# Weighing the tile that two heads share: two half-width passes replaced by two full-width passes on TensorE

## The chip, the cores and the metric

The kernel runs on one core of a Trainium2 chip. The metric is the device time of one execution in microseconds (us), the median of three runs. The engines of the core are TensorE (PE for its matmuls, PEld for its weight loads), VectorE (DVE), ScalarE (ACT), GpSimd (POOL) and SyncE (SP, which issues the DMAs). Each engine works through its own instructions in order, and waits for others by semaphores.

## What is computed

Attention with queries that are pooled over neighbouring rows, then two feed-forward layers, all with float32 inputs. Batch is 4, with 8 heads, 1152 keys and queries of 64 elements per head; pooling by 2 leaves 576 query rows per head. Cut to what matters:

```python
q_pool = q.reshape(B, H, S // 2, 2, D).mean(axis=3)
scores = (1 / sqrt(D)) * q_pool @ k.transpose(0, 1, 3, 2)
attn = exp(scores - max(scores)); attn = attn / (sum(attn) + 1e-9)
x = attn @ v                       # then (B*576, H*64) = (2304, 512)
h = x @ w_in;  x = (h * cos(h)) @ w_out          # layer 1, d_ff 2048
h = x @ w_in2; out = (h * sigmoid(h)) @ w_out2   # layer 2, d_ff 2048
```

## The kernel before

Float32 operands are split in two float16 parts, high and low, and products of the parts are summed in PSUM. Attention goes by pairs of heads (j and j + 4) of one batch: 16 pairs. The 576 rows of a head are four tiles of 128 rows and a rest of 64; the rests of the two heads are put together in one tile, number 8 (`2 * NT`), with the first head in partitions 0 to 63 and the second in 64 to 127. So a pair has nine tiles, 144 in all, of which 16 are shared ones.

A tile goes through these steps. `tile_scores` makes the scores on TensorE into PSUM tiles `sp` (L391, and for the shared tile L399, which uses half of the array's columns for each head). `tile_exp` moves them to `sc` on DVE (L410), with the row's extreme `nb` (L415), and applies the exponential on ACT (L418). `tile_hi` and `tile_lo` split the weights in `hl` (L424 on ACT, L429 on POOL), and a transposing DMA brings them to `hlT` (L431), of which there are four buffers. `tile_pv` multiplies them with the values `vt` on TensorE, in 9 chunks of 128 keys: L442 the high part with both parts of v (2 x 65 = 130 columns), L446 the low part with v's high part (65 columns). Column 64 of v's high part is one, so it gathers the sum of the weights.

Three tiles make a group and share one PSUM tile `pv`, which has a single buffer: [128, 3, 2, 65]. A pair has three groups, and the shared tile is always in the second of them. After a group's last tile, `group_end` reads `pv` on DVE: the denominators (`den`, L454), then the sum of the two halves of each slot into SBUF (`pvs`, L460), then the reciprocal (L458), which reads only `den`. Then ACT scales the rows from `pvs` into `x32`, or into `xrem` for the shared tile (L465, three instructions a group). The next group's first matmul waits until `pv` has been read.

In the shared tile, the loop of L440 takes first the 64 columns of `hlT` that belong to the first head, with that head's v, into partitions 0 to 63 of `pv`, then the other 64 columns into partitions 64 to 127. Its matmuls stand in the trace as 128*64, against 128*128 of all others but L399's.

Between the steps of attention, generators that are advanced tile by tile put in other work: loads and splitting of the next pair, splitting of the feed-forward weights, and from the fifth pair on the matmuls of layer 1 (`h`, L522; `y`, L582). The order in which each engine runs all this is set when the kernel is built: a scheduler with its own costs takes whatever has become ready, by priorities. So matmuls of different steps alternate on TensorE. After the last pair come the rest of layer 1 and the splitting of the second layer's weights, and then layer 2 (`h`, L522; `o`, L603).

## Time and profile before

| what | before |
|---|---|
| runs | 1415.83, 1414.32, 1410.59 us; median 1414.32 |
| profiled execution, first to last instruction (span) | 1411.7 us, 24909 instructions |
| attention, by the first and the last weighing matmul | 48.6 to 859.2 us |
| layer 2, TensorE without a pause of note | 1021 to 1411.7 us |

The page's time of the profiled execution is its span; the table of runs lists no other time for that execution. The median of the runs is 2.6 us above the span. In a timeline, each row gives the start, the duration, the engine, the line and the operation; a matmul's duration includes its way through the array, so what one costs its engine is the distance from its start to the next one's start.

### The profile page before, as it was taken

To read this page: it belongs to the slowest core of one execution; us is meant where nothing else is said; L and a number is where in the kernel's file an instruction comes from. 1 tells how busy PE (TensorE), PEld (TensorE's weight loads), DVE (VectorE), ACT (ScalarE), POOL (GpSimd) and SP (SyncE) were. 2 spreads that over 40 slices of the span, in tenths; PEclk is the share of its full clock that TensorE was granted. 3 is DMA by queue.
4 is the path that set the end of the run, shared out by engine and by line. 5 is a ranking of instruction groups with operands and counts; after the bars stand their busy time and mean duration, and the time that the engine had idled before them with its cause. 6 is when DMAs were issued, how large, how long until landed. Compare 5 with 4: busy or idle time off the path is not lost. (4 is left out here: it accounts for less than half of the span.)

```text
span 1411.7 us, 24909 instructions
## 1 busy us (share of the span) xinstructions
PE 1164.1 (82%) x10020; PEld 853.2 (60%) x10020; DVE 988.5 (70%) x1848; ACT 768.7 (54%) x907; POOL 568.2 (40%) x296
## 2 busy tenths in 40 slices
PE   1465356787897768898889889978899999999998
PEld 0243233475675556666667678867776666666664
DVE  7999997678678888977999985999933322223221
ACT  3686487668777678777788785555421111111110
POOL 1577276535656466646666563553600000000000
PEclk9966568799999899999999999989999999999999
DMA  7799789987799999989999964544110000000001
GB/s 232 190 238 213 186 157 206 202 167 137 149 194 171 198 205 205 176 156 185 156 208 182 220 131 86 147 120 129 52 60 31 31 6 25 31 31 16 16 2 29
DMA packets 493075, 186.17 MB, mean 132 GB/s; under 512 B 433056, under 2 KB 467872, under 8 KB 492960
## 3 DMA queue, kind: packets, MB, share of 16 engines
q1 hardware_dynamic: 492960, 184.59, 61.9%
q8 instruction: 78, 1.28, 0.4%
q14 instruction: 37, 0.30, 0.1%
HBM read 66.58 MB, written 9.44 MB: 54 GB/s over the span
## 5 line engine op out<-in xcount | busy, mean ns | idle before, releaser
L429 POOL TENSOR_TENSOR hl<-sc,hl 128x1152 f16<-128x1152 f32 x144 | 368.7, 2569 | 194.0 <-ACT hl L424 109.8
L391 PE MATMUL sp<-kT,qT 128*128 128x512 f16 (+1 forms) x768 | 196.2, 373 | 112.0 <-DVE sc L410 85.9
L535 ACT ACTIVATE hk<-h,ca 128x512 f32<-128x512 f32 x144 | 97.9, 682 | 318.0 <-PE h L522 318.0
L522 PEld LDWEIGHTS <-ih 128*128 128x128 f16 x2304 | 227.3, 100 | 66.9 <-issue 7.3
L410 DVE TENSOR_SCALAR_CACHE_REDUCE sc<-sp,psu 128x512 f32<-128x512 f32 (+1 forms) x288 | 229.0, 807 | 48.1 <-PE sp L391 46.8
L418 ACT ACTIVATE sc<-sc,nb 128x1152 f32<-128x1152 f32 x144 | 179.9, 1250 | 91.0 <-DVE nb L415 78.2
L442 PE MATMUL pv<-vt,hlT 128*128 128x130 f16 (+1 forms) x1440 | 196.1, 238 | 37.4 <-DMA hlT<-hl 29.6
L522 PE MATMUL h<-ys,ih 128*128 128x256 f16 x1152 | 196.2, 273 | 1.0 <-ACT hk L535 1.0
L522 PE MATMUL h<-xT,ih 128*128 128x256 f16 x1024 | 190.6, 280 | 2.1 <-ACT hk L535 1.3
L442 PEld LDWEIGHTS <-hlT 128*128 128x128 f16 (+1 forms) x1440 | 148.0, 111 | 67.3 <-DMA hlT<-hl 39.5
L446 PE MATMUL pv<-vt,hlT 128*128 128x65 f16 (+1 forms) x1440 | 188.4, 208 | 0.0
L391 PEld LDWEIGHTS <-qT 128*128 128x128 f16 x768 | 78.0, 110 | 180.0 <-issue 138.5
L424 ACT ACTIVATE hl<-sc 128x1152 f16<-128x1152 f32 x144 | 165.3, 1155 | 23.4 <-DMA hlT<-hl 12.2
L570 DVE TENSOR_SCALAR gh<-hk,ck 128x1024 f16<-128x1024 f32 x36 | 27.0, 751 | 206.2 <-PE o L603 198.6
L582 PE MATMUL y<-gl,oh 128*128 128x256 f16 x576 | 158.4, 275 | 2.9 <-POOL gl L563 2.9
L582 PE MATMUL y<-gh,oh 128*128 128x256 f16 x576 | 158.4, 275 | 2.1 <-ACT y L591 2.1
L582 PE MATMUL y<-gh,ol 128*128 128x256 f16 x576 | 158.4, 275 | 0.0
L522 PE MATMUL h<-ys,il 128*128 128x256 f16 x576 | 157.0, 273 | 0.0
L446 PEld LDWEIGHTS <-hlT 128*128 128x128 f16 (+1 forms) x1440 | 143.3, 108 | 15.9 <-issue 6.0
L522 PE MATMUL h<-xT,il 128*128 128x256 f16 x512 | 143.1, 280 | 0.0
L522 PEld LDWEIGHTS <-il 128*128 128x128 f16 x1152 | 114.4, 99 | 18.0 <-issue 1.3
L582 PEld LDWEIGHTS <-oh 128*128 128x128 f16 x1152 | 112.5, 99 | 20.1 <-issue 4.2
(283 smaller groups left out, 2024.5 us busy)
## 6 DMA issues: line engine op xcount, KB each, us to landing
wst<-in_moe_w_in_dram SPq DMA_DIRECT2D x16, 1024.0 KB, 5.9
wst<-in_moe_w_out_dram SPq DMA_DIRECT2D x16, 1024.0 KB, 5.9
stk<-in_k_dram SPq DMA_DIRECT2D x32, 288.0 KB, 4.3
stv<-in_v_dram SPq DMA_DIRECT2D x32, 288.0 KB, 4.4
stq<-in_q_dram SPq DMA_DIRECT2D x32, 256.0 KB, 3.1
ydr<-y SPq DMA_DIRECT2D x9, 512.0 KB, 2.9
y32b<-ydr SPq DMA_DIRECT2D x9, 512.0 KB, 3.2
out_dram<-osb SPq DMA_DIRECT2D x16, 256.0 KB, 2.1
```

The costliest lines, as they stand in the source:

```text
L391: nc.tensor.matmul(sp[:, o - a:o - a + n], P.qT[e][:, t, :], kT[:, o:o + n], start=(e == 0), stop=(e == 1))
L410: nc.vector.tensor_scalar(out=T.sc[:, a:z], in0=sp, scalar1=T.P.su, scalar2=None, op0=ALU.mult, op1=ALU.min, accum_out=mx[:, x:x + 1],)
L418: nc.scalar.activation(out=T.sc, in_=T.sc, func=AF.Exp, scale=-1.0, bias=nb)
L424: nc.scalar.activation(out=hi, in_=T.sc, func=AF.Copy)
L429: nc.gpsimd.tensor_tensor(out=T.hl[:, 1, :], in0=T.sc, in1=T.hl[:, 0, :], op=ALU.subtract)
L442: nc.tensor.matmul(G.pv[r, T.gi], T.hlT[:, 0, c, r], P.vt[i][:, c], start=(c == 0), stop=(c == KC - 1), skip_group_check=True,)
L446: nc.tensor.matmul(G.pv[r, T.gi, 0], T.hlT[:, 1, c, r], P.vt[i][:, c, 0], start=False, stop=(c == KC - 1), skip_group_check=True,)
L522: nc.tensor.matmul(hp, wt[:, c, f * 128:(f + 1) * 128], xt(c), start=(i == 0), stop=(i == 3 * NC - 1), skip_group_check=True,)
L535: nc.scalar.activation(out=o, in_=blk.hp, func=AF.Copy if first else AF.Silu, scale=blk.c.a[:, g:g + 1])
L570: nc.vector.tensor_scalar(out=gh, in0=hk, scalar1=blk.c.k, scalar2=None, op0=ALU.mult)
L582: nc.tensor.matmul(blk.y[:, oc, :], wt[:, f, oc * 128:(oc + 1) * 128], gt[:, f % 4, :], start=(f == 0 and e == 0 and oc % 2 == 0), stop=(f ...
```

## The change

The shared tile is weighed as the other tiles are, with all 128 columns of `hlT`, once with the first head's v and once with the second's. The two results go to the two halves of its slot in `pv`, where other tiles have their two partial sums. In each result only the 64 rows of its own head are wanted. The three products (high with high, high with low, low with high) are now three matmuls of 65 columns for each chunk and head, summed in one place: 54 matmuls instead of 36.

The denominators are taken for both halves of each slot (6 instead of 3 columns). ACT scales the shared tile's rows straight from `pv` in PSUM, in two instructions of 64 rows each, instead of one of 128 rows from `pvs`. The other tiles keep their matmuls; their lines now are L450 and L454, the shared tile's L443, the scaling L473 and, for the shared tile, L478.

```diff
-        hs = [(slice(0, 128), t // NT)] if t < 2 * NT else [(slice(0, 64), 0), (slice(64, 128), 1)]
-        for r, i in hs:
-            for c in range(KC):
-                nc.tensor.matmul(
-                    G.pv[r, T.gi], T.hlT[:, 0, c, r], P.vt[i][:, c],
-                    start=(c == 0), stop=(c == KC - 1), skip_group_check=True,
-                )
-                nc.tensor.matmul(
-                    G.pv[r, T.gi, 0], T.hlT[:, 1, c, r], P.vt[i][:, c, 0],
-                    start=False, stop=(c == KC - 1), skip_group_check=True,
-                )
+        if t == 2 * NT:
+            for i in range(2):
+                for c in range(KC):
+                    for e, z in ((0, 0), (0, 1), (1, 0)):
+                        nc.tensor.matmul(
+                            G.pv[:, T.gi, i], T.hlT[:, e, c], P.vt[i][:, c, z],
+                            start=(c == 0 and e == 0 and z == 0), stop=(c == KC - 1 and e == 1),
+                            skip_group_check=True,
+                        )
+            return
...
-        den = small.tile([128, GT, 1], F32, tag="den", name="den", bufs=2)
+        den = small.tile([128, GT, 2, 1], F32, tag="den", name="den", bufs=2)
...
-                nc.scalar.activation(out=dst[:, i], in_=sm[:, o + i], func=AF.Copy, scale=den[:, o + i])
+                nc.scalar.activation(out=dst[:, i], in_=sm[:, o + i], func=AF.Copy, scale=den[:, o + i, 0])
+        if 2 * NT in G.tiles:
+            o, dst = G.tiles.index(2 * NT), xrem[:, G.P.b, G.P.j * D:(G.P.j + 1) * D]
+            for i in range(2):
+                r = slice(i * 64, (i + 1) * 64)
+                nc.scalar.activation(out=dst[r], in_=G.pv[r, o, i, 0:D], func=AF.Copy, scale=den[r, o, i])
```

The scheduler runs anew, so the order moves on all engines. Three places of the twelfth pair show it (pairs are counted from 0 in the prediction: pair 11). On TensorE, inside the shared tile, before the change (`hlT` is loaded as the weights, 64 columns of it; L582 is layer 1):

```order
L446 MATMUL pv<-vt,hlT 64x65
L442 LDWEIGHTS hlT
L442 MATMUL pv<-vt,hlT 64x130
L582 LDWEIGHTS oh_83
L582 MATMUL y<-gh,oh_83 128x256
L446 LDWEIGHTS hlT
L446 MATMUL pv<-vt,hlT 64x65
L582 LDWEIGHTS oh_83
L582 MATMUL y<-gl,oh_83 128x256
```

And after the change, at the end of the first stretch of the same tile (L391 makes scores):

```order
L443 LDWEIGHTS hlT
L443 MATMUL pv<-vt,hlT 128x65
L443 LDWEIGHTS hlT
L443 MATMUL pv<-vt,hlT 128x65
L391 LDWEIGHTS qT
L391 MATMUL sp<-kT,qT 128x512
```

Before, the tile's matmuls of half width alternate one by one with matmuls of full width. After, all are of full width.

On TensorE, the start of the pair's third group, before the change (the names in brackets are the semaphores waited for; `DVE` and `Activation` stand for the engine that counts them up):

```order
L582 MATMUL y<-gh,oh_83 128x256
L442 LDWEIGHTS hlT [waits DVE_49,DMAHW6_49]
L442 MATMUL pv<-vt,hlT 128x130 [waits PE_49]
L446 LDWEIGHTS hlT
L446 MATMUL pv<-vt,hlT 128x65
```

And after:

```order
L399 MATMUL sp<-kT,qT 64x512
L450 LDWEIGHTS hlT [waits DMAHW5_49]
L450 MATMUL pv<-vt,hlT 128x130 [waits Activation_49]
L454 LDWEIGHTS hlT
L454 MATMUL pv<-vt,hlT 128x65
```

The first matmul of the third group waits for ACT now, where it waited for DVE; this is so in all 16 pairs. Other matmuls have been put ahead of it, here the scores of a shared tile.

On ACT, the end of the second group of that pair, before the change (`x` and `xrem` hold the scaled rows):

```order
L424 ACTIVATE hl<-sc 128x1152 [waits DMAHW6_49,Activation_49]
L465 ACTIVATE x_5195<-pvs,den 128x64 [waits DVE_49]
L465 ACTIVATE xrem<-pvs,den 128x64
L465 ACTIVATE x_5196<-pvs,den 128x64
L418 ACTIVATE sc<-sc,nb 128x1152 [waits DVE_49,Pool_49] x2
```

And after:

```order
L424 ACTIVATE hl<-sc 128x1152 [waits DMAHW5_49,Activation_49]
L473 ACTIVATE x_5347<-pvs,den 128x64 [waits DVE_49]
L473 ACTIVATE x_5348<-pvs,den 128x64
L478 ACTIVATE xrem<-pv,den 64x64 [waits PE_49]
L478 ACTIVATE xrem<-pv,den 64x64
L418 ACTIVATE sc<-sc,nb 128x1152 [waits DVE_49,Pool_49] x2
```

The two instructions that read `pv` stand last of the four, behind the two that read `pvs`.

## Rows read from the trace of the kernel before

**Rows 1.** The page: busy time of each engine; busy tenths in 40 slices.

```profile
PE 1164.1 (82%) x10020; PEld 853.2 (60%) x10020; DVE 988.5 (70%) x1848; ACT 768.7 (54%) x907; POOL 568.2 (40%) x296
PE   1465356787897768898889889978899999999998
DVE  7999997678678888977999985999933322223221
```

**Rows 2.** Stretches: length; busy us of each engine (instructions); clock; DMA.

```profile
45.00:275.00 230.00, 127.01 (x1032) 81.57 (x1031) 208.38 (x438) 157.86 (x177) 141.99 (x73) 0.71 0.96 199
275.00:600.00 325.00, 267.23 (x2703) 204.14 (x2702) 266.37 (x538) 245.69 (x292) 185.27 (x102) 0.95 0.93 178
600.00:860.00 260.00, 233.16 (x2356) 178.93 (x2355) 221.25 (x421) 194.28 (x235) 152.10 (x77) 0.97 0.89 175
1021.00:1412.00 391.00, 384.42 (x2680) 261.76 (x2679) 110.95 (x155) 60.65 (x85) 2.23 (x2) 1.00 0.07 25
```

**Rows 3.** Stretches, as rows 2, around and behind two of the shared tiles.

```profile
600.00:618.00 18.00, 18.00 (x137) 11.37 (x135) 11.23 (x23) 11.51 (x12) 11.20 (x8) 1.00 0.81 170
...
801.60:814.70 13.10, 13.10 (x125) 9.65 (x124) 13.10 (x23) 8.23 (x11) 7.13 (x4) 0.99 0.80 151
...
sum 82.80, PE 82.80 PEld 59.26 DVE 63.31 ACT 52.20 POOL 48.01; mean PE 13.80 PEld 9.88 DVE 10.55 ACT 8.70 POOL 8.00
```

**Rows 4.** Timeline of PE in a full tile: start us, duration us, operation.

```profile
653.15 0.22 PE L442 MATMUL pv<-vt,hlT 128*128 128x130 f16 x1
653.21 0.27 PE L582 MATMUL y<-gh,oh 128*128 128x256 f16 x1
653.32 0.19 PE L446 MATMUL pv<-vt,hlT 128*128 128x65 f16 x1
653.35 0.28 PE L582 MATMUL y<-gl,oh 128*128 128x256 f16 x1
```

**Rows 5.** Timeline of PE in the shared tile of pair 11.

```profile
656.12 0.22 PE L442 MATMUL pv<-vt,hlT 128*64 128x130 f16 x1
656.19 0.19 PE L446 MATMUL pv<-vt,hlT 128*64 128x65 f16 x1
656.22 0.22 PE L442 MATMUL pv<-vt,hlT 128*64 128x130 f16 x1
656.37 0.28 PE L582 MATMUL y<-gh,oh 128*128 128x256 f16 x1
656.58 0.22 PE L446 MATMUL pv<-vt,hlT 128*64 128x65 f16 x1
656.73 0.28 PE L582 MATMUL y<-gl,oh 128*128 128x256 f16 x1
656.94 0.24 PE L442 MATMUL pv<-vt,hlT 128*64 128x130 f16 x1
```

**Rows 6.** Timeline at the end of pair 14's second group: DVE, PE, ACT.

```profile
814.50 0.54 DVE L460 TENSOR_REDUCE pvs<-pv 128x192 f32<-128x384 f32 x1
819.54 0.16 DVE L458 RECIPROCAL den<-den 128x3 f32<-128x3 f32 x1
815.94 0.22 PE L442 MATMUL pv<-vt,hlT 128*128 128x130 f16 x1
820.95 0.33 ACT L465 ACTIVATE xrem<-pvs,den 128x64 f32<-128x64 f32 x1
821.19 0.33 ACT L465 ACTIVATE x<-pvs,den 128x64 f32<-128x64 f32 x1
```

**Rows 7.** The same of pair 1, PE and ACT.

```profile
135.34 0.27 PE L442 MATMUL pv<-vt,hlT 128*128 128x130 f16 x1 [0.87 <-DVE pvs L460]
136.94 0.33 ACT L465 ACTIVATE x<-pvs,den 128x64 f32<-128x64 f32 x1
```

**Rows 8.** Waits of PE, whole span: us in total, times, longest.

```profile
PE sp L391 <- DVE sc L410: 85.9, 63, 4.8
PE pv L442 <- DVE den L458: 5.7, 2, 4.2
```

More of the change, by code (lines that the diff above doesn't have):

```diff
@@ L438, in tile_pv @@
             G.pv = at.ps_v.tile([128, GT, 2, D + 1], F32, tag="pv", name="pv")
-        hs = [(slice(0, 128), t // NT)] if t < 2 * NT else [(slice(0, 64), 0), (slice(64, 128), 1)]
-        for r, i in hs:
-            for c in range(KC):
-                nc.tensor.matmul(
-                    G.pv[r, T.gi], T.hlT[:, 0, c, r], P.vt[i][:, c],
-                    start=(c == 0), stop=(c == KC - 1), skip_group_check=True,
-                )
-                nc.tensor.matmul(
-                    G.pv[r, T.gi, 0], T.hlT[:, 1, c, r], P.vt[i][:, c, 0],
-                    start=False, stop=(c == KC - 1), skip_group_check=True,
-                )
+        if t == 2 * NT:
[8 more added lines that the diff above has]
+            return
+        for c in range(KC):
+            nc.tensor.matmul(
+                G.pv[:, T.gi], T.hlT[:, 0, c], P.vt[t // NT][:, c],
+                start=(c == 0), stop=(c == KC - 1), skip_group_check=True,
+            )
+            nc.tensor.matmul(
+                G.pv[:, T.gi, 0], T.hlT[:, 1, c], P.vt[t // NT][:, c, 0],
+                start=False, stop=(c == KC - 1), skip_group_check=True,
+            )
     def group_end(at, G, n, dsts):
-        den = small.tile([128, GT, 1], F32, tag="den", name="den", bufs=2)
+        den = small.tile([128, GT, 2, 1], F32, tag="den", name="den", bufs=2)
         nc.vector.tensor_scalar(
-            out=den[:, 0:n], in0=G.pv[:, 0:n, 0, D:D + 1], scalar1=1e-9 * 2.0**PSH, scalar2=G.P.s[:, 2:3],
+            out=den[:, 0:n], in0=G.pv[:, 0:n, :, D:D + 1], scalar1=1e-9 * 2.0**PSH, scalar2=G.P.s[:, 2:3],
             op0=ALU.add, op1=ALU.mult,
@@ L763, in drain_pv @@
                 if t == 2 * NT:
-                    dsts.append((o, 1, xrem[:, b:b + 1, j * D:(j + 1) * D]))
                     continue
```

## Prediction, on record before the changed kernel ran

> **What bounds the kernel now.** I read the slices first [rows 1]: TensorE is busy to nine tenths and more in the last ten, and between five and nine tenths before. The stretches [rows 2] say which engine leads where. In layer 2, 1021 to 1412 us, TensorE is busy 384.42 of 391 us; the change touches nothing there, so its effect has to arise before 860 us. In 45 to 275 us DVE leads with 208.38 of 230 us and TensorE has 127.01, so time given to or taken from TensorE counts little. In 275 to 600 us TensorE (267.23 of 325) and DVE (266.37) stand level. In 600 to 860 us TensorE leads with 233.16 of 260 us, that is 0.90, and DVE has 221.25. The stages after attention begin when it has ended, so I carry what attention gains or loses to the end unchanged.
>
> **What is removed: changes of width.** A matmul's cost is the distance to the next start. Where a full tile alternates with layer 1 [rows 4], 130 columns cost 0.06 us (653.15 to 653.21), 256 columns 0.11 and 65 columns 0.03. In the shared tile [rows 5], as long as half-width matmuls follow each other, the steps are the same: 656.12, 656.19, 656.22. Where they alternate with full-width ones, 130 columns take 0.15 us, then 256 columns 0.21, 65 columns 0.15, 256 columns 0.21. So each change of width costs 0.09, 0.10, 0.12 and 0.10 us more than the step itself: 0.105 us on average. In the order of the kernel before, TensorE changes width 224 times at the weighing of the 16 shared tiles; by the tile it is 2 to 56 times. 224 x 0.105 = 23.5 us of TensorE's time go.
>
> How much of that was on the path? Six tiles (pairs 5, 10, 11, 12, 14 and 15) hold 180 of the 224 changes. From their start to some 7 us behind their end TensorE has no pause: 82.80 of 82.80 us over the six stretches [rows 3]. There every change delays what comes next. In the stretch of pair 14, though, DVE is busy 13.10 of 13.10 us too [rows 3]; its 24 changes I count at nothing. The other 156 are worth 16.4 us, and I take TensorE's share of 600 to 860 us, 0.90, of them: **-14.7 us**. The remaining 44 changes (4.6 us) lie mostly where TensorE waits for others anyway, DVE above all [rows 2, 8]; I take a quarter, **-1.2 us**.
>
> The scores of the shared tile keep their half width (L399). Their changes of width fall from 80 to 60 in the new order, because the scheduler placed them otherwise: 20 x 0.105 = 2.1 us of TensorE's time, of which I take half, **-1.0 us**.
>
> **What is added on TensorE.** The columns are the same: 36 matmuls of before are 18 x 130 + 18 x 65 = 3510 columns, the 54 of after are 54 x 65 = 3510. A weight load stands before each matmul, 54 now for 36. Before, a 65-column matmul takes 0.03 us although the next weight load falls under it [rows 4, 5], so a load is hidden under 65 columns; the trace shows no two of these in a row. From below the price is nothing; from above I bound it by the mean of one 130-column and one 65-column step, (0.06 + 0.03) / 2 = 0.045 us for each of 54, that is 2.4 us instead of 1.6 us a tile, +0.8 us, and +13 us for 16. I take **0**, since the 65-column step itself is the nearest row; no reason speaks for a gain.
>
> The Trainium skill has two rules that speak against the change. "TensorE: Matmul & The Clock Gate", section "Back-to-back issue gap", gives a sustained roofline of about 81 ns for pairs of weight load and matmul at 128 columns; by that 54 pairs would take 4.4 us a tile, an estimate, and 16 tiles +45 us. The trace disagrees so far, with 0.09 us for two such pairs [rows 4]. "TensorEngine Tiling (Array Packing)", section "Key Properties", says that tiles of the array work independently and in parallel; by that the two half-width passes of before could have run at once in half of 1.6 us, and the change would give that up, 0.8 x 16 = +13 us. Here they did not: the halves follow each other, and their steps are those of full-width matmuls [rows 4, 5].
>
> **What is added elsewhere.** ACT runs four scaling instructions instead of three in 16 groups; they follow each other at 0.24 us [rows 6], so 16 x 0.24 = 3.9 us more for ACT, which is busy 54% [rows 1]. That the two new ones read PSUM and 64 rows is not in the trace; I bound them by nothing and by twice the row, +8 us of ACT. The new order has 47 table loads for 49, which gives some of it back. On the path I take **0**, hidden by ACT's pauses. The denominators have 6 columns for 3, next to nothing in a 0.16 us instruction [rows 6]; **0**.
>
> **The wait that is added.** `pv` has one buffer. Before, it came free when DVE had summed it: in pair 14 at 815.04 us, and the third group's first matmul started at 815.94 [rows 6]. After, ACT's two instructions have to have read it as well, and they stand behind the reciprocal (819.54) and two others of ACT; in the trace of before the last of the three scalings ends at 821.52, 5.58 us after that matmul's start [rows 6]. In pair 1 it is 137.27 against 135.34 us, 1.93 us late [rows 7]. So it is in 11 of the 16 pairs, from pair 1 to pair 14, and the 11 sum to 34.4 us; in the other five ACT is done before. With the fourth instruction (some 0.5 us until it ends, 11 times 0.5 = 5.5) the matmul would have to start 40 us later in all. Behind it in TensorE's queue stand the third group's tiles, scores that DVE waits for, and layer 1.
>
> Yet the scheduler knows of the wait and has moved matmuls ahead of it. Between the last matmul of the second group and the first of the third, the other matmuls, at 0.11 us for 256 columns [rows 4] and in proportion, come to 46.5 us over the 16 pairs before and to 80.1 us after: 33.6 us have been moved in front, and the third group's tiles run closer together behind it. 40 - 34 = 6 us are left as pauses: **+6 us**. From below it is 0, where TensorE's other waits cover it; from above 40 us, where the moved matmuls are not ready either.
>
> **The sum.** -14.7 - 1.2 - 1.0 + 0 + 0 + 6 = -10.9 us against the span of 1411.7 us: 1400.8 us. The runs' median stands 2.6 us above the span, so 1414.3 - 10.9 = **1403 us**.
>
> **The rivals.**
>
> *The wait for ACT decides, and the kernel gets slower.* The place is the first matmul of each pair's third group. For it speaks that ACT comes late in 11 of 16 pairs already, and that DVE waits for the scores queued behind; TensorE waits 85.9 us for DVE [rows 8], and a loop of two engines that wait for each other gives a delay on. Against it speaks the moved work, and that TensorE waited only 5.7 us for a `pv` in this way before [rows 8]. If the moved matmuls stood in for nothing, 40 - 17 = +23 us, 1437 us; if for half of the 40, 20 - 17 = +3 us. It decides from about 17 us of pauses at this place, and is over half a per cent slower from 24 us. Chance 0.13.
>
> *The gain is absorbed.* TensorE is through the shared tile sooner, and then waits longer for DVE to free the scores' PSUM. For it: in 275 to 600 us DVE is as busy as TensorE, and 221.25 us of 600 to 860 [rows 2]. Against it: the six stretches without a pause, where DVE has 63.31 of 82.80 us [rows 3]. Then a third of the 23.5 us arrives, -8, and the wait for ACT takes 6: -2, 1412 us. Chance 0.22.
>
> *The change does not do what it says on TensorE*, since a weight load does not hide under 65 columns. At 0.045 us a matmul it costs +13 us of TensorE's time, and the sum comes to about +1 us, 1415 us. Chance 0.05.
>
> *A load and a matmul take much longer still.* At 0.08 us for each of 54 matmuls, more than any step of 65 or 130 columns within a full tile [rows 4], the tile takes 4.3 us for 1.6, 16 times 2.7 = +43 us, and at 0.9 of it +39 - 11 = +28 us, 1442 us. That is what the skill's first rule above would make of it. The rows of 0.03 us speak against it: chance 0.02.
>
> **How the numbers follow.** The forecast has 0.58, absorbed 0.22, weight loads 0.05, the wait for ACT 0.13, the longest loads 0.02. The forecast's own range goes from all changes of width on the path and no pause (23.5 + 2.1 = 25.6 us less, 1389 us) to about 1407. The range that holds 8 in 10 takes in absorbed and weight loads and the lower part of the wait for ACT: 1389 to 1419 us. A measurement of this kernel can tell about half a per cent, 7 us, from no change: faster is below 1407, slower above 1421. To faster go the forecast, 0.58, and 0.03 of absorbed; to slower 0.11 of the wait for ACT and the 0.02; the rest, 0.26, is the same.
>
> **What would show it.** In the profile of the changed kernel, the steps within a shared tile should read 0.03 us for 65 columns, and no step of 0.15 to 0.21 us should stand there. TensorE's busy time should fall from 1164 us by about 20 to 25 us. A wait of the first weighing matmul for ACT should appear with 5 to 10 us in all; if it has over 17 us the first rival is right. If TensorE's wait for DVE at L391 rises from 85.9 us by about as much as its busy time falls, the gain was absorbed. Layer 2 should take the same 391 us, and start some 11 us earlier than 1021 us. The prediction is wrong if attention ends no earlier than before although TensorE is busy 20 us less, or if the new order moved other work onto the path.

## The result, and the profile after

The changed kernel takes **1421.21 us** (median of 6 runs, 1417.80 to 1429.91) against 1412.41 us for the kernel before (6 runs, 1410.59 to 1415.83): ratio **1.0073**, 95% interval 1.0048 to 1.0097. The ratio and its interval are worked out from all runs; the quotient of two medians can differ from it by 0.1 to 0.2%, here 1.0062. The kernel is slower by 0.7%, where 1403 us and a range up to 1419 had been predicted. The profiled execution took 1419.03 us, with a span of 1417.0 us.

The page's busy times (they answer [rows 1]):

```profile
PE 1147.5 (81%) x10308; PEld 853.3 (60%) x10308; DVE 996.1 (70%) x1848; ACT 774.2 (55%) x921; POOL 562.3 (40%) x296
```

TensorE has 16.6 us less to do than before (1164.1), and the end is 5.3 us later (1411.7 to 1417.0). So TensorE stands still for 22 us more. The last weighing matmul starts at 864.3 us, where it started at 859.0, although TensorE has less to do; the prediction had named this as a sign of being wrong. The stretches, with the same columns as [rows 2]; the last one is layer 2:

```profile
45.00:275.00 230.00, 117.33 (x1080) 77.80 (x1079) 206.81 (x434) 155.57 (x176) 140.00 (x72) 0.75 0.94 196
275.00:600.00 325.00, 262.99 (x2797) 205.25 (x2798) 273.68 (x533) 247.76 (x297) 185.99 (x101) 0.93 0.95 177
600.00:860.00 260.00, 223.07 (x2443) 175.92 (x2440) 220.27 (x421) 198.02 (x240) 149.49 (x78) 0.95 0.94 176
1026.00:1417.00 391.00, 385.80 (x2696) 263.13 (x2693) 110.56 (x155) 58.78 (x83) 3.75 (x2) 1.00 0.07 25
```

Layer 2 takes the same 391 us, so the loss lies ahead of it. In 275 to 600 us VectorE now leads with 273.68 us (before 266.37), and the clock is lower in both attention stretches: 0.93 and 0.95, where [rows 2] have 0.95 and 0.97. The waits of TensorE, whole span (us in total, times, longest), answer [rows 8]:

```profile
PE sp L391 <- DVE sc L410: 93.4, 80, 4.9
...
PE pv L450 <- DMA hlT<-hl: 35.5, 21, 3.8
PE sp L391 <- DMA kT<-kn: 30.3, 6, 12.8
...
PE pv L450 <- DVE pvs L468: 7.9, 5, 2.6
...
PE pv L443 <- DMA hlT<-hl: 2.6, 2, 1.4
...
PE pv L450 <- ACT xrem L478: 1.6, 1, 1.6
```

Before, the wait for the transposed weights read

```profile
PE pv L442 <- DMA hlT<-hl: 29.6, 22, 3.7
```

Four waits grew by 27 us in all: for the transposed weights 8.5 us more (29.6 to 35.5 + 2.6), for VectorE's readings of the scores 7.5 us more (85.9 to 93.4), for VectorE's sum of the weighed tiles 6.0 us more (1.9 to 7.9), for the transposed keys 5.3 us more (25.0 to 30.3). The wait for the denominators (5.7 us before) is gone in return, which leaves the further 22 us. The wait for ACT, which the prediction feared, is 1.6 us. What the full width does on the array, and one place where its gain goes, is seen at the shared tile of pair 11, TensorE alone (start, duration, operation; "x18" stands for 18 matmuls in a row):

```profile
657.01 0.72 PE L443 MATMUL pv<-vt,hlT 128*128 128x65 f16 x18
660.38 1.13 PE L391 MATMUL sp<-kT,qT 128*128 128x512 f16 x4 [2.65 <-DVE sc L410]
661.30 0.98 PE L443 MATMUL pv<-vt,hlT 128*128 128x65 f16 x14
...
663.68 0.26 PE L443 MATMUL pv<-vt,hlT 128*128 128x65 f16 x1
663.75 0.36 PE L595 MATMUL y<-gh,oh 128*128 128x256 f16 x1
663.94 0.19 PE L443 MATMUL pv<-vt,hlT 128*128 128x65 f16 x1
663.97 0.27 PE L595 MATMUL y<-gl,oh 128*128 128x256 f16 x1
664.08 0.19 PE L443 MATMUL pv<-vt,hlT 128*128 128x65 f16 x1
```

The steps are what was predicted: from 663.94 on, 65 columns cost 0.03 us and 256 columns 0.11 us, although layer 1 alternates with the tile; the 0.15 and 0.21 us of [rows 5] are gone. But TensorE then waits 2.65 us for VectorE inside this very tile, and at 663.68 the 65 columns take 0.07 us: there the granted clock is at the lower level, 1.2 GHz. The 18 steps ahead of the pause still take 0.03 us each (0.72 us with the last one's way through the array); behind the pause the clock has fallen. In the kernel before TensorE had no pause in this tile.

### The profile page after: what moved, and what is told of

Its sections match the earlier page's. It is cut to its first block, busy times and chain, and to the rows that moved or that the text cites. A ratio compares the mean times of both kernels' runs of the same rounds, so it can differ in the third digit from the quotient of the medians.

```text
span 1417.0 us, 25472 instructions
## 1 busy us (share of the span) xinstructions
PE 1147.5 (81%) x10308; PEld 853.3 (60%) x10308; DVE 996.1 (70%) x1848; ACT 774.2 (55%) x921; POOL 562.3 (40%) x296
## 5 line engine op out<-in xcount | busy, mean ns | idle before, releaser
L391 PE MATMUL sp<-kT,qT 128*128 128x512 f16 (+1 forms) x768 | 193.1, 371 | 124.2 <-DVE sc L410 93.4
L450 PE MATMUL pv<-vt,hlT 128*128 128x130 f16 x1152 | 154.0, 236 | 45.8 <-DMA hlT<-hl 35.5
L391 PEld LDWEIGHTS <-qT 128*128 128x128 f16 x768 | 78.3, 109 | 183.2 <-issue 137.3
L595 PE MATMUL y<-gh,oh 128*128 128x256 f16 x576 | 161.7, 281 | 3.5 <-ACT y L604 3.5
L595 PE MATMUL y<-gl,oh 128*128 128x256 f16 x576 | 161.7, 281 | 0.0
L595 PE MATMUL y<-gh,ol 128*128 128x256 f16 x576 | 161.5, 280 | 0.0
L450 PEld LDWEIGHTS <-hlT 128*128 128x128 f16 x1152 | 118.2, 108 | 68.0 <-DMA hlT<-hl 44.2
L454 PE MATMUL pv<-vt,hlT 128*128 128x65 f16 x1152 | 146.9, 207 | 0.0
L454 PEld LDWEIGHTS <-hlT 128*128 128x128 f16 x1152 | 114.2, 105 | 8.2 <-issue 4.6
```

What stands on the lines that cost most here:

```text
L391: nc.tensor.matmul(sp[:, o - a:o - a + n], P.qT[e][:, t, :], kT[:, o:o + n], start=(e == 0), stop=(e == 1))
L450: nc.tensor.matmul(G.pv[:, T.gi], T.hlT[:, 0, c], P.vt[t // NT][:, c], start=(c == 0), stop=(c == KC - 1), skip_group_check=True,)
L454: nc.tensor.matmul(G.pv[:, T.gi, 0], T.hlT[:, 1, c], P.vt[t // NT][:, c, 0], start=False, stop=(c == KC - 1), skip_group_check=True,)
L595: nc.tensor.matmul(blk.y[:, oc, :], wt[:, f, oc * 128:(oc + 1) * 128], gt[:, f % 4, :], start=(f == 0 and e == 0 and oc % 2 == 0), stop=(f ...
```

## The experiments

**How an order is kept.** Any edit lets the scheduler put all instructions in another order. To change one thing at a time, most kernels below write the order down, each engine's list taken from the kernel before ("old order") or from the changed kernel ("new order"); each instruction follows the one before it on its engine by a dependency without a semaphore:

```diff
+                if before is not None:
+                    tc.add_manual_dep(
+                        i, before.name, mybir.DependencyInfo(mybir.DependencyClass.NoSync, mybir.DependencyReason.DATA),
+                        reason="kept order",
+                    )
+                before = i
```

All ratios are against the kernel before on the same chip, with 95% intervals; 0.001 is 1.4 us. Several kernels leave something out, so that their output is wrong; their expectations say so. Three theories were on record: the removed changes of width are worth what was predicted and the new order gives it back (first theory); the gain is absorbed, as TensorE waits longer and its clock falls (second); ACT's reading of `pv` costs it (third).

### What the order costs, what the width gives

| work | old order | new order |
|---|---|---|
| that of before | 1 | 1.0134 [1.0098, 1.0171] |
| full width in 54 steps, VectorE reads `pv` alone | 0.9965 [0.9948, 0.9981] | 1.0066 [1.0042, 1.0091] |
| that of the changed kernel | 1.0084 [1.0069, 1.0098] | 1.0073 [1.0048, 1.0097], the changed kernel |
| the same, ACT's readings placed earlier | 1.0006 [0.9990, 1.0021] | 1.0087 [1.0063, 1.0110] |
| that of the changed kernel, half width | | 1.0144 [1.0121, 1.0166] |

**work_of_before_new_order**: the kernel before, with the changed kernel's order.

> The work of the kernel before (narrow steps, VectorE reads the PSUM tile alone), every engine in the order of the changed kernel. Theory 'the new order costs by itself': 1417 to 1426, up to 1.009 of before. Theory 'the new order costs only by ACT's readings': 1409 to 1416.

Measured: 1433.03 us, 1.0134. The new order costs 14 to 24 us by itself with the work of before. It also makes that work's changes of width more frequent: at the weighing of the shared tiles the trace has 274 of them, for 224 in the old order. The 50 more are worth 5 us of TensorE's time at the prediction's 0.105 us. The second row of the table has no such changes in either order: there the new order costs 1.0066 against 0.9965, 1.0%.

**full_width_54_steps_new_order**:

```diff
+                if t == 2 * NT:
+                    for e, z in ((0, 0), (0, 1), (1, 0)):
+                        nc.tensor.matmul(
+                            G.pv[:, T.gi, z], T.hlT[:, e, c], P.vt[i][:, c, z],
```

> The work of full_width_54_steps_old_order (0.9965 of before there; the shared tile's output rows are wrong), every engine in the order of the changed kernel; it differs from the changed kernel by ACT's two readings alone, in whose place one scaling reads VectorE's sum. Theory 'the new order costs by itself and covers ACT's readings': 1416 to 1421, as the changed kernel. Theory 'ACT's readings cost in this order too': 1404 to 1411.

Measured: 1421.15 us, 1.0066: within 0.001 of the changed kernel. In the new order ACT's two readings of PSUM cost nothing beyond the intervals (0.25% to either side of each); and against the 1.0134 above, the full width gives 0.7%, 9.6 us.

**half_width_new_order**: the changed kernel, of each head's steps only the first chunk at full width.

```diff
+                        r = slice(i * 64, (i + 1) * 64) if c else slice(0, 128)
-                            G.pv[:, T.gi, i], T.hlT[:, e, c], P.vt[i][:, c, z],
+                            G.pv[r, T.gi, i], T.hlT[:, e, c, r], P.vt[i][:, c, z],
```

> The changed kernel, with every engine's instructions kept in exactly the order of the changed kernel, and one edit: in the shared tile, 8 of the 9 chunks take only the 64 columns of their own head (the first chunk stays full, so that all rows of pv are written). So the width changes of the weighing come back, in the new order, which has fewer of them than the old one (about 60 at the edges of the stretches and inside). Theory 1: 3 to 8 us slower than the changed kernel, 1424 to 1429, since width changes cost path time in any order. Theory 2: the same as the changed kernel, 1419 to 1423. Theory 3 says nothing on it beyond theory 1.

Measured: 1430.77 us, 1.0144, 0.7% above the changed kernel: the same worth of the width by another pair of kernels. The count in the expectation was wrong, though. The trace has 340 changes of width at the weighing, not about 60, and TensorE is busy 1186.7 us, 39 us more than in the changed kernel (1147.5). So the first theory's half on the width doesn't hold in this order either: of 274 x 0.105 = 29 us and 340 x 0.105 = 36 us of TensorE's time some 10 us arrive, about a third. Its half on the order does.

**other_order_alone**: another edit that leaves the work as it is.

```diff
-        den = small.tile([128, GT, 1], F32, tag="den", name="den", bufs=2)
+        den = small.tile([128, GT, 2, 1], F32, tag="den", name="den", bufs=2)
...
-            out=den[:, 0:n], in0=G.pv[:, 0:n, 0, D:D + 1], scalar1=1e-9 * 2.0**PSH, scalar2=G.P.s[:, 2:3],
+            out=den[:, 0:n], in0=G.pv[:, 0:n, :, D:D + 1], scalar1=1e-9 * 2.0**PSH, scalar2=G.P.s[:, 2:3],
```

> The kernel before with one small edit that leaves the work as it is (the reciprocal is taken of 6 columns in place of 3, 12 ns or so on VectorE) and lets the scheduler put the instructions in another order of its own, as any edit does. Theory 'the order by itself moves the time by several us': outside 1409 to 1415, to either side by up to 10 us. Theory 'the order is nearly free': within 1410 to 1415.

Measured: 1420.12 us, 1.0047 [1.0028, 1.0067]. A third order, without any of the change, is slower than that of before too. It has 278 changes of width at the weighing for 224, so part of the loss can be theirs.

**Where the new order loses.** The traces of before and of work_of_before_new_order hold the same instructions but for two table loads of ACT. TensorE's waits in the latter, whole span:

```profile
PE sp L391 <- DVE sc L410: 86.4, 71, 4.9
PE sp L391 <- DMA kT<-kn: 30.2, 5, 13.1
...
PE pv L442 <- DVE pvs L460: 11.1, 5, 4.0
```

Before, the second and the third read 25.0 and 1.9 us:

```profile
PE sp L391 <- DMA kT<-kn: 25.0, 5, 13.5
...
PE pv L442 <- DVE pvs L460: 1.9, 2, 1.0
```

The wait for the scores' readings is as before (86.4 for 85.9 us); the wait for the keys (`kT`) and the one for the sum (`pvs`) have grown. One place explains most of the growth for the keys. It is the start of pair 3, where VectorE splits the new keys (`kn`, L311) ahead of their transpose. Before, VectorE:

```profile
242.08 0.16 DVE L458 RECIPROCAL den<-den 128x3 f32<-128x3 f32 x1
242.17 1.51 DVE L311 SCALAR_TENSOR_TENSOR kn<-stk,ps__1907,kn 128x576 f16<-128x576 f32 x2
243.60 0.81 DVE L311 SCALAR_TENSOR_TENSOR vt<-stv,ps__1907,vt 128x576 f16<-128x576 f32 x1
```

Then VectorE in the new order, and under it POOL there:

```profile
243.76 2.21 DVE L311 SCALAR_TENSOR_TENSOR kn<-stk,ps__1907,kn 128x576 f16<-128x576 f32 x1
245.89 2.48 DVE L355 COPY qn<-qn 128x576 f16<-128x576 f16 x1
248.29 0.80 DVE L311 SCALAR_TENSOR_TENSOR kn<-stk,ps__1907,kn 128x576 f16<-128x576 f32 x1
```

```profile
242.98 5.21 POOL L429 TENSOR_TENSOR hl<-sc,hl 128x1152 f16<-128x1152 f32 x2 [5.65 <-DVE qn L352]
```

The new order reaches the keys 1.6 us later and puts the copy of the queries between their two halves. With that, the first half and the copy run beside POOL's subtraction (242.98 to 248.19); before, the keys were done when POOL began at 243.70. The split takes 2.21 us for 0.8, the copy 2.48 us, where the 16 copies of this line before (ns: shortest, median, longest) read

```profile
L355 DVE COPY qn<-qn x16: 309/316/2476, 15.4 to 770.5; 128x576 f16<-128x576 f16 x16
```

The keys are ready at 249.1 instead of 243.7, and their transpose is issued 6.5 us later (SP's queue, before and in the new order):

```profile
244.62 3.08 SPq L367 DMA_TRANSPOSE kT<-kn  x1
```

```profile
251.13 2.59 SPq L367 DMA_TRANSPOSE kT<-kn  x1
```

TensorE waits 9.2 us for it, before 4.7; the changed kernel waits 8.2 us at this place. VectorE's sum of the pair's last group ends at 277.1 us instead of 270.3; that of the pair before had ended 1.1 us late. But this delay doesn't last: the sum of the first group of pair 5 ends at 367.3 us instead of 366.1. From there the lag grows again in pieces, to 12.4 us at the last group of attention (873.6 instead of 861.2). So the place shows how an order makes VectorE's work longer; it isn't the place where the whole loss comes from.

The Trainium skill says of this, in "SBUF — State Buffer", section "SBUF: two separate sides", that VectorE and GpSimd share a pair of ports, which VectorE takes for instructions in a two-port mode and, against a GpSimd instruction that reads SBUF, for those with two inputs in SBUF; whichever instruction comes first holds the pair for its whole length while the other is blocked. By that the split and the copy wait for POOL; the trace agrees, as the copy ends at 248.37, right behind POOL (248.19).

The profiled execution of work_of_before_new_order, with a span of 1422.9 us, is faster than the runs' median, so the trace shows 11 us of the loss and not all of it. Two further differences: the weighed tiles' sum comes later (the wait for `pvs` above), and VectorE's same 1848 instructions take 998.1 us instead of 988.5. How much of the loss each makes is not shown. The clock falls too: in 865 to 1046 us, columns as above, before and in the changed kernel,

```profile
865.00:1046.00 181.00, 158.82 (x1377) 136.57 (x1375) 151.30 (x218) 95.12 (x107) 76.97 (x29) 0.96 0.36 104
```

```profile
865.00:1046.00 181.00, 162.56 (x1382) 140.06 (x1381) 148.49 (x222) 94.57 (x108) 76.30 (x29) 0.93 0.35 103
```

With a mean of c in a stretch of T us, (1 - c) x T / 0.5 us of it are at 1.2 GHz: over 275 to 600, 600 to 860 and 865 to 1046 us that is 33 + 16 + 14 = 63 us before and 46 + 26 + 25 = 97 us in the changed kernel. A column takes twice as long there, so up to 17 us of TensorE's own time is lost. It is an upper bound, since TensorE is not always busy there, and in 45 to 275 us it is the other way (0.71 before, 0.75 after). The order alone has less of it: in work_of_before_new_order the same three stretches have 0.93, 0.98 and 0.93, which is 81 us at 1.2 GHz. No run holds the clock fixed, so how much of the order's cost comes by it stays open.

### Why the width gives so little in the old order

| VectorE's sum of the weighed tiles (old order) | narrow steps | full width |
|---|---|---|
| as before, 545 ns | 1 | 0.9970 [0.9954, 0.9986] |
| of one tile, 277 ns | 0.9998 [0.9980, 1.0015] | 0.9916 [0.9893, 0.9940] |
| by PSUM, VectorE only copies | 1.0050 [1.0035, 1.0066] | 0.9990 [0.9970, 1.0009] |

**full_width_old_order**:

```diff
-                    G.pv[r, T.gi], T.hlT[:, 0, c, r], P.vt[i][:, c],
-                    start=(c == 0), stop=(c == KC - 1), skip_group_check=True,
+                    G.pv[:, T.gi], T.hlT[:, 0, c], P.vt[i][:, c],
+                    start=(c == 0 and r.start == 0), stop=(c == KC - 1), skip_group_check=True,
```

> The kernel before, with every engine's instructions kept in exactly the order of the kernel before, and one edit: the shared tile's 36 matmuls take all 128 columns of the weights and write all 128 rows, the second head's on top of the first's (so the shared tile's 64-row blocks are left wrong; nothing else is left out). No width change is left at the weighing, the reading of pv is DVE's as before, and no order moves. Theory 1 (the removed width changes are worth what was predicted, and the new order gave it back): 10 to 17 us faster than before, 1396 to 1402. Theory 2 (the gain is absorbed, TensorE only waits longer and its clock falls): within 4 us of before, 1408 to 1416. Theory 3 (the reading of pv by ACT costs it): as theory 1, 1396 to 1402.

Measured: 1409.06 us, 0.9970. TensorE's busy time falls by 15.9 us (1148.2), and 4 us of it arrive. TensorE's wait for the scores is 92.4 us, 6.5 more than [rows 8], and takes up the larger part of what is missing:

```profile
PE sp L391 <- DVE sc L410: 92.4, 65, 5.2
```

**full_width_54_steps_old_order**: as its new-order twin above, old order.

> The kernel before with the order of its instructions kept on every engine; the shared tile is weighed by the whole array, both heads' results in the same place (so its output rows are wrong), but in 54 steps of 65 columns as in the changed kernel, in place of 36 of 130 and 65. VectorE and ACT do what they did before. To be set beside full_width_old_order (1409.06 us), which differs by the 18 more steps and weight loads for each shared tile alone. Theory 'the steps are free' (what the prediction said of the 54 weight loads): within 2 us of 1409, so 1407 to 1411. Theory 'the steps cost': 16 tiles with 18 more instructions each; by the difference of 7 us between full_width_read_by_dve_old_order and full_width_old_order, of which they would then be the larger part, 1413 to 1417.

Measured: 1408.36 us, 0.9965. The 18 more steps and weight loads of each tile are free.

**one_head_weighed_old_order**:

```diff
-        hs = [(slice(0, 128), t // NT)] if t < 2 * NT else [(slice(0, 64), 0), (slice(64, 128), 1)]
+        hs = [(slice(0, 128), t // NT)] if t < 2 * NT else [(slice(0, 128), 0)]
```

(on top of full_width_old_order)

> full_width_old_order with the second head's 18 steps of each shared tile left out (its output rows are wrong; 288 steps fewer): TensorE has some 18 x 16 steps less, at about 0.045 us each 13 us of busy time less at the high clock, beside the 16 us that full_width_old_order had already lost. Theory 'TensorE's work in the attention sets the time': 13 us less than full_width_old_order, 1394 to 1398. Theory 'work taken from TensorE there comes back as waits for VectorE's readings of the scores and as a lower granted clock': 2 to 6 us less, 1403 to 1408, with TensorE's wait for VectorE's sc readings above the 88 us of full_width_old_order by 4 us or more.

Measured: 1407.11 us, 0.9960 [0.9945, 0.9976]. Half of the tile's work is gone, TensorE's busy time falls by another 11.1 us (1137.1), and the time stays that of full_width_old_order within the intervals. Two waits take it up, each with about half: the one for the scores (5.7 us more) and the one for the transposed weights (28.3 us there, 5.9 us more here):

```profile
PE sp L391 <- DVE sc L410: 98.1, 72, 4.8
...
PE pv L442 <- DMA hlT<-hl: 34.2, 25, 5.4
```

**short_sum_old_order**:

```diff
-            out=sm[:, 0:n], in_=G.pv[:, 0:n, :, 0:D].rearrange("p n z d -> p n d z"), axis=AX.X, op=ALU.add
+            out=sm[:, 0:1], in_=G.pv[:, 0:1, :, 0:D].rearrange("p n z d -> p n d z"), axis=AX.X, op=ALU.add
...
-                nc.scalar.activation(out=dst[:, i], in_=sm[:, o + i], func=AF.Copy, scale=den[:, o + i])
+                nc.scalar.activation(out=dst[:, i], in_=sm[:, 0], func=AF.Copy, scale=den[:, o + i])
```

> The kernel before, order of all instructions kept, with VectorE's sum of the two halves of the weighed tiles (545 ns, 48 times) cut to one of the three tiles (its output is wrong; some 0.3 us less for each group, 15 us of VectorE in all, and the PSUM tile is free that much earlier). TensorE's work is that of before, narrow steps included. Theory 'VectorE sets the pace of the attention, TensorE's narrow steps hardly': the time falls by about as much as VectorE's work, 10 to 15 us, to 1397 to 1403. Theory 'TensorE sets it': at most 4 us, 1408 to 1412. Theory 'whatever is gained goes back through the granted clock': 1408 to 1412 as well, with 8 us or more of further time at the low clock between 275 and 865 us.

Measured: 1414.30 us, 0.9998. I had expected VectorE to set the pace; 48 x 0.268 = 12.9 us less of this sum, and the PSUM tile free that much sooner, give nothing. VectorE as a whole was hardly relieved, though:

```profile
PE 1159.7 (82%) x10020; PEld 850.3 (60%) x10020; DVE 986.9 (70%) x1848; ACT 768.6 (54%) x907; POOL 571.4 (40%) x296
```

Its busy time is 986.9 us for 988.5. Other instructions took longer in return: the 32 splits of the values (`vt`, L311) 48.4 us in all, before 37.3. So this run doesn't show what a VectorE with less to do would give.

**short_sum_full_width_old_order**: both edits.

> full_width_old_order (1409.06 us) with the same cut of VectorE's sum as in short_sum_old_order. The two give the worth of the changes of width once VectorE is relieved. Theory 'VectorE sets the pace': as short_sum_old_order or up to 6 us faster, since TensorE's 16 us can now count: 1392 to 1400. Theory 'what is gained goes back through the granted clock': 1403 to 1409.

Measured: 1401.94 us, 0.9916. The short sum alone gives 0.0%, the full width alone 0.3%, both 0.8%. That is more than the two gains added, by more than the intervals. With the short sum, the width is worth 0.82%, 11.6 us. Here VectorE's busy time did fall, from 991.8 us (full_width_old_order) to 977.3. One reading is that neither engine alone bounds the attention: they pass scores to each other through the same PSUM tiles, each hides what the other saves, and a gain arrives when both get it. A rival is that the short sum was eaten up by VectorE's longer splits in the one profiled execution and not in the other; no run tells the two apart. What full_width_old_order and one_head_weighed_old_order do show for the second theory is that the gain is absorbed: TensorE's waits, those for VectorE's readings first, grow as its work shrinks.

### What ACT's reading of PSUM costs

**new_work_old_order**: the changed kernel, old order.

> The changed kernel's work in the order of the kernel before: three 65-column matmuls stand where a 130- and a 65-column one stood, ACT's two readings of pv where the one scaling of the shared tile stood, all else in the old places. Theory 1 (the order gave the gain back): faster than the changed kernel, with the wait of TensorE for ACT not covered by moved work: minus 15 for the width changes, plus 5 to 20 for the wait, 1402 to 1417. Theory 2 (absorbed): before plus the wait for ACT, 1415 to 1430. Theory 3 (ACT's reading costs it): the wait is as long as the trace of before says, 30 to 40 us at the first matmul of the third groups, and the kernel slower than the changed one, 1425 to 1437.

Measured: 1424.57 us, 1.0084. TensorE's wait for ACT is there as the prediction had worked it out (34.4 us in 11 pairs if nothing covers it); in the whole span it reads:

```profile
PE pv L450 <- ACT xrem L478: 36.5, 12, 7.1
```

**act_reads_pv_old_order**: full_width_old_order, with only the reading changed.

```diff
+        if 2 * NT in G.tiles:
+            o, dst = G.tiles.index(2 * NT), xrem[:, G.P.b, G.P.j * D:(G.P.j + 1) * D]
+            for i in range(2):
+                r = slice(i * 64, (i + 1) * 64)
+                nc.scalar.activation(out=dst[r], in_=G.pv[r, o, i, 0:D], func=AF.Copy, scale=den[r, o])
```

> The kernel before with the order of its instructions kept on every engine; the shared tile is weighed by the whole array in 36 steps as in full_width_old_order (1409.06 us), and its two halves are read from the PSUM tile by two scalings on ACT, as in the changed kernel (without adding the small part of the weights' product, so its output rows are wrong). It differs from full_width_old_order by ACT's reading alone. Theory 'the reading by ACT costs': TensorE waits for ACT at the first weighing of a group some 11 times for 3 us as in new_work_old_order (35.1 us of waits there), and the time is that of full_width_old_order plus the 8 us between new_work_old_order and full_width_read_by_dve_old_order: 1415 to 1420. Theory 'the waits for ACT only take the place of other waits': 1408 to 1412.

Measured: 1424.33 us, 1.0083 [1.0062, 1.0105]: with the old order the reading costs 1.1%, 16 us, more than I had expected, and is all that the new work loses there.

**new_work_readings_first_old_order**: new_work_old_order, the five lines above moved ahead of the loop of scalings. **new_work_readings_before_exp_old_order**: the same, and the two readings one more place ahead in ACT's list, which in most groups is ahead of an exponential.

> new_work_old_order (1424.57 us) with ACT's two readings of the shared tile put ahead of the scaling that waits for VectorE's sum, in place of behind it: the PSUM tile is free some 0.7 us earlier at each of 16 groups. Theory 'the reading costs by its lateness': 11 to 16 groups times 0.7 us, less 8 to 11 us: 1413 to 1417. Theory 'the reading costs whenever it stands in ACT's queue behind an exponential of 1.25 us': the wait stays, 1420 to 1424.

> As new_work_readings_first_old_order, and the two readings also stand one instruction earlier in ACT's queue, ahead of the exponential (or copy) behind which they stood at 14 of 16 groups. Theory 'the reading costs by its lateness': another 1 us or so at 8 to 14 groups, to 1403 to 1412, the time of the full width with the reading for nothing. Rival: the exponential now waits for VectorE's reciprocal, and the weights of a later tile come late: 1415 to 1425, with more waits of TensorE for the transposed weights (hlT).

Measured: 1420.86 us, 1.0042 [1.0024, 1.0061], and 1414.61 us, 1.0006 [0.9990, 1.0021]. Each move gives 5 to 6 us. The first one hardly brings the readings forward in its trace: from the end of VectorE's sum to the end of the readings it is 54.2 us over the 16 groups in new_work_old_order and 53.6 us here, and TensorE's wait for ACT stays (36.9 us). So its gain isn't explained by that wait. The second one does (38.2 us), and leaves 21.5 us of the wait:

```profile
PE pv L450 <- ACT xrem L475: 21.5, 9, 5.6
```

So in the old order the lateness costs, since TensorE's list has nothing to do meanwhile; the second move shows it, the first doesn't.

**readings_early_in_new_order**: the changed kernel, the readings ahead of their group's scalings and, at 12 groups, of one more instruction.

> The changed kernel with its own order kept on every engine, but ACT's two readings of the shared tile ahead of the two scalings of their group, and at 12 of 16 groups ahead of the exponential or copy before those too. Theory 'the reading costs by its lateness, in this order too': as in the old order, where the same move gave 10 us, to 1411 to 1416. Theory 'in the new order other work covers the lateness (TensorE waits only 1.6 us for ACT in the trace of after), and the loss is the order's own, like the 6.6 us of other_order_alone': 1418 to 1422.

Measured: 1426.14 us, 1.0087: nothing is gained over the changed kernel. There the moved matmuls cover the lateness already (1.6 us of wait for ACT). So the third theory holds in the old order alone.

**full_width_read_by_dve_old_order**: the new steps, with VectorE copying the shared tile's two halves.

```diff
+            for i in range(2):
+                r = slice(i * 64, (i + 1) * 64)
+                nc.vector.tensor_copy(sm[r, o], G.pv[r, o, i, 0:D])
+            nc.vector.tensor_copy(den[64:128, o, 0], den[64:128, o, 1])
```

> The full-width weighing of the changed kernel, but pv is read by DVE alone (a sum over the two other slots, two copies of 64 rows for the shared one, and one copy of its denominators, in place of the sum over three), ACT has its three scalings as before, and the order of the kernel before is kept. Computes the reference. DVE gets about 16 x 0.4 = 6 us more work. Theories 1 and 3: 6 to 15 us faster than before, 1398 to 1407. Theory 2: 1410 to 1418.

Measured: 1416.27 us, 1.0029 [1.0013, 1.0044]. Against the 0.9965 without the copies that is 9 us, for 0.45 us more of VectorE in each of 16 groups (a sum of two tiles 414 ns, two copies of 217 and one of 150, for one sum of 545), 7 us in all. So VectorE's time is not free in this kernel.

### A version that beats both?

The products can be summed where they are made: three steps of 65 columns into one place for every tile, a place of its own for the second head, and VectorE copies 192 or 256 columns in place of the sum.

```diff
+        for o, i in [(T.gi, t // NT)] if t < 2 * NT else [(T.gi, 0), (GT, 1)]:
+            for c in range(KC):
+                for e, z in ((0, 0), (0, 1), (1, 0)):
+                    nc.tensor.matmul(
+                        G.pv[:, o], T.hlT[:, e, c], P.vt[i][:, c, z],
...
+        nc.vector.tensor_copy(sm[:, 0:m], G.pv[:, 0:m, 0:D])
```

> The kernel before, old order, with the three products of a tile (130 and 65 columns before) weighed in three steps of 65 columns into one place, so that PSUM makes the sum of the two halves and VectorE only copies 192 columns (some 0.25 us less for each of 48 groups, 12 us in all); the shared tile is still weighed in the two halves of the array. Computes the reference. Theory 'either engine alone hides the other' (from short_sum_old_order, 0.9998 of before): 1408 to 1415. Theory 'VectorE sets the pace': 1398 to 1405. 1440 more TensorE steps and weight loads stand against it, free by full_width_54_steps_old_order.

> As sum_in_psum_narrow_old_order, with the shared tile weighed by the whole array, once with each head's v, in two places of the PSUM tile, which VectorE copies with the others; ACT's two scalings read the copy and not the PSUM tile. Computes the reference. Theory 'either engine alone hides the other': as short_sum_full_width_old_order, 1399 to 1405, 8 to 13 us below the narrow one. Theory 'the shared tile's width is worth 4 us at most': 1405 to 1411.

> sum_in_psum_full_width_old_order in the order that the scheduler gives it of itself. An order by itself moved the time by some 7 us (other_order_alone), so by the theory 'either engine alone hides the other' 1395 to 1411; above 1412 would say that the order that it gets takes back the whole gain.

Measured: 1420.23 us, 1.0050; 1413.19 us, 0.9990; 1434.41 us, 1.0135 [1.0106, 1.0165]. The width is worth 0.6% here, 8 us, and that part of the expectation held; the level did not, it is 0.5 and 0.7% above the runs with the short sum. VectorE's copy takes 0.35 us, more than the short sum's 0.28, and the full tiles have three steps where they had two; which of these it is was not tried. With the scheduler's own order the same work takes 21 us more than in the old one. No kernel that does the whole work was faster than the one before beyond its interval.

## Why the prediction was wrong

- **Steps.** Right. The steps of 65 columns take 0.03 us, and no step of 0.15 to 0.21 us follows a change of width at the weighing. The Trainium skill's "TensorEngine Tiling (Array Packing)", section "Key Properties", says in words that switching the tiling mode drains TensorE. The trace agrees in that each change costs time, and gives the number: 0.09 to 0.12 us [rows 5].
- **The weight loads, +0.** Right: 0.9965 with 54 steps, 0.9970 with 36.
- **-14.7 and -1.2 us for the changes of width.** The size on TensorE was two thirds right (its busy time fell by 15.9 us in the old order and 16.6 us in the changed kernel, where 20 to 25 us had been forecast), the way to the end was not. I took the six stretches without a pause [rows 3] as proof that nine tenths would arrive. Measured are -0.35% or 4.9 us in the old order, -0.7% or 9.6 us in the new one, and -0.8% with the short sum. A stretch in which TensorE has no pause shows that no wait shows up yet; what is next late after a gain, VectorE's readings of the scores and the transposed weights, is not seen in it. So this term failed too: 14.7 + 1.2 us had been forecast to arrive, 4.9 to 9.6 us did. (The four values that the 0.105 us is said to be the mean of give 0.1025, 23 us in all instead of 23.5.) The rival "absorbed" had the mechanism, and with a third of the gain, 8 us of 23.5, also the size.
- **+0 for ACT and +6 us for the wait.** The mechanism was right, the size too high in the new order: 1.6 us of waits, and 1.0073 against 1.0066 in time. With the old order the wait is there in full and costs 16 us, so the moved work was rightly named as its cover.
- **The step that failed: the moved work was counted only as a gain.** I read from the new order what it does between the second and the third group (33.6 us moved in front) and to the scores' changes of width (-1.0), and gave the rest of it no price. The order by itself costs +1.0% with the full-width work and +1.3% with that of before, 14 to 19 us, and turns the forecast gain into a loss. The text's last sentence names this ("or if the new order moved other work onto the path"), without a price and without a chance among the rivals.

The sum with what was measured, in parts of the time before: order +1.34%, full width in 54 steps -0.68%, ACT's readings +0.07%, together +0.73%. Taken in the other sequence, width first, it is -0.35% for the width in the old order, +1.01% for the order, and +0.07%. Each term is the difference of two runs with intervals of 0.2 to 0.4% to either side, so each term is good to some 6 us. That the order is the largest term, and the signs of order and width, are clear; the sign of ACT's readings is not. The scores' changes of width (-1.0) were not tried apart.

## What to carry to other kernels

In a kernel whose order comes from a scheduler, an edit is two changes, the work and the order; keep the old order with the new work, and the new order with the old work, before you credit or blame the edit. Where two engines work level, price a gain of one by what the other hands it next, not by the first one's busy share. A buffer's new reader costs its lateness behind its own queue, unless the order gives the waiting engine other work.

## What was not expected of the hardware

The same VectorE instructions have very different lengths by what POOL does beside them: 0.31 to 2.48 us for one copy of 576 columns, 0.80 to 2.21 us for one split. So what runs beside what decides how long VectorE's work is, and the order only in part. In three orders the 1848 instructions took 988.5, 998.1 and, in other_order_alone, 1002.5 us; with the old order kept, they took 988.5 to 998.6 us in kernels whose work for VectorE is nearly the same (998.6 in new_work_old_order).

In the changed kernel TensorE has 16.6 us less to do, and 97 us between 275 and 1046 us were at 1.2 GHz instead of 63. The runs make no rule of this: in short_sum_full_width_old_order TensorE is busy 26 us less than before (1137.7), and the clocks of 0.95, 0.97 and 0.94 in the same three stretches make 70 us.
